# A fused SSD and GELU kernel: the long decay rows loaded from the GpSimd queue, w_out moved ahead in the load order, and a new order of all steps

## The chip, the cores and the metric

The kernel runs on one core of a Trainium2 chip. The metric is the device time of one launch in microseconds, as the median of repeated runs. The profile comes from one further execution, whose own time is given beside its span.

## The reference

Two stages follow each other. The first is a chunked state space recurrence over 4 batches, 8 heads and 768 positions with 32 values a head (`D`) and a state of 16 (`N`); the second is a feed-forward layer with a tanh-GELU on 3072 tokens of 256 values.

```python
cum = np.cumsum(la, axis=-1)
L = np.exp(cum[:, :, :, None] - cum[:, :, None, :])
...
CB = np.einsum('bhin,bhjn->bhij', Cc, Bc)
M = CB * L
y_intra = np.einsum('bhij,bhjd->bhid', M, xc)
decay_to_i = np.exp(cum)
y_inter = np.einsum('bhin,bhnd->bhid', Cc, state) * decay_to_i[:, :, :, None]
y[:, :, sl] = y_intra + y_inter
state = decay_full[:, :, None, None] * state + np.sum(Bx, axis=2)
...
h = x @ w_in
g = 0.5 * h * (1.0 + np.tanh(c * (h + 0.044715 * h * h * h)))
return (g @ w_out).astype(np.float32)
```

`a` (the decays) is needed before `B` and `C` can be scaled, these before any chunk can be computed, and `w_in` and `w_out` before its tokens can go through the feed-forward layer. The state runs through the 6 chunks of a batch in order.

## The kernel before, in words

The sequence is cut into 24 chunks of 128 positions, six for each batch. The first four chunks are units of their own (unit 0 to 3), the later ones go in pairs (units 4 to 13). Unit 4 holds the last two chunks of batch 0, units 5 to 7 are batch 1, and so on.

**Decays.** The rows of `a` for batch 0 come early and in short pieces (`a3_t`, two halves); those for batches 1 to 3 are the long rows, `a12_t`: `load_a12` (L164) brings them in four DMAs of 32 rows with 384 values, through `load_a` (L156, L157). VectorE clips them (`f_clip12`, L305), scans them into running products (`f_R12`, L301), transposes (`f_RT12`, L327) and takes reciprocals for each batch (L331).

**B and C.** Batch 0 comes in halves (`load_bc3`, L259); its scaled copies are made on VectorE (`f_mul3`, L361) and transposed on TensorE (`f_T3`, L372). Batches 1 to 3 come by `load_bc` (L153): B into the lower 64 partitions of one tile `bc_t`, C into the upper 64. One VectorE step `f_mul` (L400) scales both, so it needs both loads and the long decay rows; TensorE then transposes (`f_T`, L408), the results are copied out of PSUM (`f_E`), C is masked (`f_F`, L419), and B is transposed once more (`f_N`, L427, and `f_bn`).

**A unit** then takes `f_castx` (x to bf16), `f_G` (C times B, L462), `f_M` (the causal mask, VectorE, L472), `f_D` (the chunk's own state, L483), `f_S` (the running state, VectorE, L530 and L532), `f_SP` (the masked state, L539), `f_Y` (L505 from the state, L514 from the chunk itself) and `f_yev` (its copy to `xm`).

**Feed-forward.** `f_s1` (L563) multiplies by `w_in`, in groups that fill one PSUM bank: 8 matmuls of 128 columns for units 0 to 3, 4 matmuls of 256 columns later. ScalarE applies the GELU (L572). `f_s2` (L581) multiplies by `w_out`, 16 matmuls of 256 columns to a chunk, four of them to each quarter of `w_out`. `f_oev` (L588, L590) and `f_store` (L594) bring the result out. `w_in` (two loads of 1024 KB, L276) and `w_out` (four loads of 512 KB, L282) arrive in float32 in a pool of three buffers and are cast to bf16 in pieces of 512 columns on GpSimd or ScalarE (L288, L286).

**PSUM.** Groups of `f_s1` and the results of `f_D` share two banks (`hp`), so a result of `f_D` that VectorE has not read yet holds one of the two.

**The order.** No engine chooses at run time: each works off its own list in order. The lists come from a planner in the kernel (`run_order`), a list scheduler over nodes with an engine, an assumed duration, dependencies and a priority. The table `TUNE` overrides the priority of each node, `ENG` chooses the engine of those that have a choice, and the list `FIRST` with the loop after it gives the loads. All loads except six DMAs for `a3_t` on the ScalarE queue, and all stores, are issued from SyncE (SP), in the planner's order. Before the first `f_s1` group the planner fills idle TensorE time with dummy matmuls (L843).

Of the kernel before, what the change touches and what calls it, by code (L numbers as in the profile page):

```python
# [93 lines left out]
def kernel(  # L94
# [10 lines left out]
    nc = tc.nc  # L105
# [6 lines left out]
    HS = S // 2  # L112
    R3 = HS // 128
    R12 = S // 64
# [29 lines left out]
    a12_t = const.tile([128, HS], FP32, name="a12_t")  # L144
# [11 lines left out]
    def load_a(eng, o, at, n):  # L156
        eng.dma_start(out=o, in_=bass.AP(tensor=a.tensor, offset=a.offset + at,  # L157
                                         ap=[[S, batch * H], [1, n]]))
# [2 lines left out]
        n = ES if q == 3 else 2 * ES  # L161
        load_a(eng, a3_t[32 * q:32 * q + 32, i, 0:n], i * HS + q * ES, n)

    def load_a12():  # L164
        for q in range(4):
            load_a(nc.sync, a12_t[32 * q:32 * q + 32], (q % 2) * HS, HS)

    nc.vector.memset(a3_t[96:128, :, ES:], 1.0)
    for q in range(4):
# [424 lines left out]
        nc.sync.dma_start(out=out[gc * Q:(gc + 1) * Q, :], in_=outs.pop(gc))  # L594


    TUNE, ENG = {'ad_bc3_0_1': 14.089, 'ad_bc3_0_0': 14.0678, 'ad_wi_0': 14.1187, 'ad_x_0': 14.1183, 'ad_wi_1': 14.1056, 'ad_x_1': 14.1439, 'ad_bc3_1_1': 14.1458, 'ad_bc3_1_0': 14.1953, 'ad_x_2': 14.1853, 'ad_wo_0': 14.2062, 'ad_x_3': 14.2092, 'ad_wo_1': 14.2112, 'ad_wo_2': 14.2017, 'ad_wo_3': 14.2126, 'ad_a12': 14.1975, 'ad_x_4': 14.2621, 'ad_x_5': 14.2618, 'ad_bc_1_1': 14.2284, 'ad_bc_1_0': 14.2513, 'ad_x_6': 14.2822, 'ad_x_7': 14.3073, 'ad_x_8': 14.268, 'ad_x_9': 14.3453, 'ad_x_10': 14.2846, 'ad_x_11': 14.3005, 'ad_bc_2_1': 14.3163, 'wi_0_0': 21.0405, 'wi_0_1': 20.9083, 'wo_0_0': 20.9265, 'wo_0_1': 20.9062, 'wi_1_0': 20.9749, 'wi_1_1': 21.089, 'wo_1_0': 21.0332, 'wo_1_1': 20.9149, 'wi_2_0': 20.9485, 'wi_2_1': 21.0163, 'wo_2_0': 20.9335, 'wo_2_1': 20.9078, 'wi_3_0': 21.1114, 'wi_3_1': 20.9955, 'wo_3_0': 21.0099, 'wo_3_1': 21.0181, 'clip3_0': 21.0288, 'R3_0': 20.8079, 'RT3_0': 21.0102, 'recip3_0': 20.8186, 'mul3_0_1': 20.8335, 'mul3_0_0': 21.0695, 'pe_0': 20.7716, 'pp_0': 1064.0232, 'pend_0': 21.0365, 'clip3_1': 20.9727, 'R3_1': 21.0804, 'RT3_1': 21.0354, 'recip3_1': 21.0755, 'mul3_1_1': 21.0261, 'mul3_1_0': 20.899, 'pe_1': 21.012, 'pp_1': 1064.0555, 'pend_1': 20.9371, 'clip12': 20.9832, 'R12': 21.0475, 'RT12': 21.0619, 'recip12_1': 20.9625, 'recip12_2': 21.0472, 'recip12_3': 20.9963, 'castx_0': 21.0575, 'T3_0_1': 1064.1412, 'T3_0_0': 1064.0195, 'F0_0_0': 21.036, 'F0_0_1': 20.8627, 'E0_0': 20.8832, 'N_0_0': 1064.1682, 'bn_0_0': 20.789, 'G_0': 1064.1163, 'D_0': 1064.1738, 'M_0_0_0_2': 20.7953, 'M_0_0_2_4': 20.7659, 'S_0_0': 21.0221, 'SP_0': 21.0373, 'Y_0': 1064.1445, 'yev_0': 20.9328, 'castx_1': 20.9236, 'D_1': 1064.0368, 'M_1_0_0_4': 21.0544, 'S_1_0': 21.0483, 'SP_1': 21.0557, 'Y_1': 1064.1909, 'yev_1': 21.0776, 'castx_2': 20.9245, 'mul_1': 20.9712, 'T_1': 1063.9923, 'E_1_1': 20.9532, 'E_1_0': 20.8862, 'F_1': 21.0349, 'N_1': 1063.9691, 'G_2': 1064.0079, 'D_2': 1064.0093, 'M_2_0_0_4': 21.0354, 'S_2_0': 20.9225, 'SP_2': 21.0259, 'Y_2': 1064.1286, 'yev_2': 20.9261, 'castx_3': 20.9184, 'T3_1_1': 1064.0633, 'T3_1_0': 1063.994, 'F0_1_0': 20.9141, 'F0_1_1': 20.8485, 'E0_1': 21.0213, 'N_0_1': 1064.0256, 'bn_0_1': 21.0085, 'G_3': 1064.1608, 'D_3': 1063.9226, 'M_3_0_0_4': 21.0212, 'S_3_0': 20.9855, 'SP_3': 21.0435, 'Y_3': 1063.985, 'yev_3': 20.9136, 'castx_4': 20.9264, 'G_4': 1063.9808, 'D_4': 1063.9849, 'M_4_0_0_4': 20.9883, 'M_4_1_0_4': 21.0103, 'S_4_0': 21.0953, 'SP_4': 21.0283, 'Y_4': 1063.946, 'yev_4': 20.8422, 'castx_5': 20.8662, 'castx_6': 20.836, 'castx_7': 21.0818, 's1_0_0': 1064.0449, 'gelu_0_0': 20.8915, 's1_0_1': 1064.0631, 'gelu_0_1': 20.9213, 's1_0_2': 1064.0272, 'gelu_0_2': 20.8905, 's1_0_3': 1064.006, 'gelu_0_3': 21.0468, 's1_1_0': 1063.9464, 'gelu_1_0': 20.9289, 's1_1_1': 1064.0345, 'gelu_1_1': 20.8626, 's1_1_2': 1063.9974, 'gelu_1_2': 20.9102, 's1_1_3': 1063.8997, 'gelu_1_3': 20.8815, 's1_2_0': 1063.9713, 'gelu_2_0': 20.902, 's1_2_1': 1064.0101, 'gelu_2_1': 20.7947, 's1_2_2': 1063.9829, 'gelu_2_2': 20.8536, 's1_2_3': 1064.0064, 'gelu_2_3': 20.8901, 's1_3_0': 1063.9973, 'gelu_3_0': 20.9096, 's1_3_1': 1063.9988, 'gelu_3_1': 20.9607, 's1_3_2': 1063.9747, 'gelu_3_2': 20.9292, 's1_3_3': 1064.0169, 'gelu_3_3': 20.9948, 's1_4_0': 1063.8964, 'gelu_4_0': 20.9401, 's1_4_1': 1063.7613, 's2_0_0_0_o': 1064.1635, 's2_0_0_1_o': 1064.0266, 's2_0_0_2_o': 1064.0006, 's2_0_0_3_o': 1064.1858, 'oev_0': 20.8721, 's2_1_0_0_o': 1063.9561, 's2_1_0_1_o': 1063.9453, 's2_1_0_2_o': 1064.0086, 's2_1_0_3_o': 1064.0111, 'oev_1': 20.8661, 's2_2_0_0_o': 1063.9328, 's2_2_0_1_o': 1063.9913, 's2_2_0_2_o': 1064.0311, 's2_2_0_3_o': 1063.9668, 'oev_2': 21.0387, 's2_3_0_0_o': 1063.8998, 's2_3_0_1_o': 1063.8525, 's2_3_0_2_o': 1063.8591}, {'wi_0_1': 'ACT', 'wi_1_0': 'ACT', 'wo_1_1': 'ACT', 'wi_2_0': 'ACT', 'wo_2_0': 'ACT', 'wi_3_1': 'ACT', 'castx_0': 'ACT', 'F0_0_0': 'DVE', 'F0_0_1': 'DVE', 'E0_0': 'ACT', 'bn_0_0': 'DVE', 'castx_1': 'ACT', 'yev_1': 'DVE', 'E_1_1': 'ACT', 'E_1_0': 'ACT', 'bn_0_1': 'DVE', 'oev_2': 'DVE'}
    MERGE = UOF[CPB]
    TAIL = 4
    nodes = []  # L600
# [1 line left out]
    def add(eng, dur, fn, *args, deps=(), prio=0.0, done=None):  # L602

        name = "_".join([fn.__name__[2:]] + [str(v) for v in args])
        opts = eng if isinstance(eng, dict) else None
        if opts:
            eng = ENG.get(name, next(iter(opts)))
            dur = opts[eng]
            args = args + (eng,)
        n = Node(eng, dur, (lambda: fn(*args)), deps, TUNE.get(name, prio),  # L610
                 (0.26 if eng == "PE" else 0.0) if done is None else done)
        n.name, n.opts = name, opts
        nodes.append(n)
        return n
# [7 lines left out]
    def load(dur, fn, *args, deps=()):  # L622
        nload[0] += 1
        return add("DMA", dur, fn, *args, deps=deps, done=0.9, prio=nload[0])

    win_l, won_l, wi_n, wo_n = {}, {}, {}, {}
# [5 lines left out]
    a3n.done = 0.8  # L632
    a3n1 = add("SP", 7.2, landed, "a1", done=0.9, prio=-1)

    FIRST = "C30 B30 i0 x0 i1 x1 C31 B31 x2 o0 x3 o1 o2 o3 A x4 x5"
    for item in FIRST.split() + [f"{t}{b}" if t in "CB" else f"x{CPB * b + int(t)}"
                                 for b in range(1, batch) for t in "CB012345"]:
        t, i = item[0], int(item[1:] or 0)
        if t in "CB" and i >= 30:
            bl3[i - 30, int(t == "C")] = load(1.2, load_bc3, i - 30, int(t == "C"))  # L640
        elif t in "CB":
            bl[i, int(t == "C")] = load(1.2, load_bc, i, int(t == "C"))
        elif t == "A":
            a12n = load(1.7, load_a12)
        elif t == "x":
            xl[i] = load(1.0, load_x, i)
        elif t == "i":
            win_l[i] = load(2.65, load_wi, i)
        else:
            won_l[i] = load(1.35, load_wo, i)  # L650
# [11 lines left out]
    for k in range(2):  # L662
        z = 60.0 * k
        cl3n[k] = cl3 = add("DVE", 0.27, f_clip3, k, deps=[(a3n, a3n1)[k]], prio=-98 + z)
        R3n[k] = add("DVE", 0.55, f_R3, k, deps=[cl3], prio=-97 + z)
        RT3n[k] = add("DVE", 0.28, f_RT3, k, deps=[R3n[k]], prio=-96 + z)
        rc3[k] = add("DVE", 0.26, f_recip3, k, deps=[RT3n[k]], prio=-95 + z)
        mul3[k, 1] = add("DVE", 0.5, f_mul3, k, 1, deps=[bl3[k, 1], rc3[k]], prio=-94 + z)
        mul3[k, 0] = add("DVE", 0.5, f_mul3, k, 0, deps=[bl3[k, 0], RT3n[k]], prio=-93 + z)
        pen = add("DVE", 0.4, f_pe, k, deps=[R3n[k]], prio=-60 + z / 2)  # L670
        ppn = add("PE", 0.4, f_pp, k, deps=[pen], prio=-28)
        pendn[k] = add("ACT", 0.2, f_pend, k, deps=[ppn], prio=-29)
        ppn.takes("hp", pendn[k])
    cl12 = add("DVE", 0.42, f_clip12, deps=[a12n], prio=60)
    R12n = add("DVE", 1.08, f_R12, deps=[cl12], prio=60)
    RT12n = add("DVE", 1.02, f_RT12, deps=[R12n], prio=60)
# [44 lines left out]
    for u, cs in enumerate(UNITS):  # L721
        n = len(cs)
        q = 10.0 * cs[0]
# [16 lines left out]
        for k in range(n):  # L740
# [3 lines left out]
            else:  # L744
                ms.append(add("DVE", 1.24, f_M, u, k, 0, 4, deps=[gn] + ms,
                              prio=q + 1 + 0.1 * k if u > 1 else -16 + 2 * u + 0.1 * k))
# [8 lines left out]
        for k, gc in enumerate(cs):  # L755
            if gc % CPB == CPB - 1:
# [4 lines left out]
                          prio=q + 1.5 + 0.1 * k if u > 1 else -13.5 + u)  # L761
# [13 lines left out]
    for u, cs in enumerate(UNITS):  # L775
# [3 lines left out]
        for i in range(4 * n):  # L779
# [3 lines left out]
                              prio=PB + 10 * c0)  # L783
# [96 lines left out]
```

## Time and profile before

| | |
|---|---|
| median of 13 runs | 125.46 us (123.38 to 126.31) |
| time of the profiled execution | 126.11 us |
| its span, first to last instruction | 123.9 us |
| TensorE busy (matmul) | 112.2 us, 91% |
| ScalarE busy | 77.7 us, 63% |
| VectorE busy | 68.0 us, 55% |
| GpSimd busy | 17.4 us, 14% |
| read from HBM, written to it | 10.85 MB, 3.15 MB |
| the 24 x loads, each | 128 KB, median 4.7 us from issue to landing |
| the four w_out loads, each | 512 KB, median 5.7 us from issue to landing |
| the four loads of the long decay rows, each | 48 KB, median 2.1 us from issue to landing |
| clock granted to TensorE | full speed throughout |

The difference of the profiled execution's time to its span, 2.2 us, lies ahead of the first and after the last instruction. Engines with a "q" (SPq, PEq) are sequencers, which issue DMAs and wait. A wait is the idle time of an engine ahead of an instruction, with what ended it. The chain of waits is followed backwards from the last instruction, at each step to what released it.

### The profile page before, as it was taken

How to read it: one execution, taken by the hardware profiler on the slowest of the kernel's cores; microseconds unless marked ns; L12 is line 12 of the kernel's file. 1: busy time of each engine (PE TensorE's matmuls, PEld its weight loads, DVE VectorE, ACT ScalarE, POOL GpSimd, SP SyncE). 2: the span in 40 equal slices, each digit the busy share in tenths (PEclk: the TensorE clock that was granted, in tenths of full speed). 3: DMA queues.
4: the chain of work that ended last, by engine and by line, in shares of the span. 5: the costliest groups of instructions: out<-in, count | busy, mean ns of one | idle time of the engine just before them, and what ended most of it. 6: DMA issues, size and time to landing. Idle time of an engine off the chain costs nothing.

```text
span 123.9 us, 3597 instructions
## 1 busy us (share of the span) xinstructions
PE 112.2 (91%) x1537; PEld 98.8 (80%) x1537; DVE 68.0 (55%) x127; ACT 77.7 (63%) x150; POOL 17.4 (14%) x36
## 2 busy tenths in 40 slices
PE   5967997669899959999999999999999999999980
PEld 5946877468688848999888997979898899999960
DVE  5769979963939297852699461747557200000110
ACT  0516989464675647859766676776576877668510
POOL 7103506331331051011100000000000000000000
PEclk9999999999999999999999999999999999999999
DMA  1999979996879699995011101110111011111021
GB/s 41 204 366 354 160 212 330 320 200 108 162 187 227 111 163 240 149 166 138 0 42 48 42 0 48 42 45 3 45 42 48 7 40 42 42 42 42 9 81 42
DMA packets 37199, 14.23 MB, mean 115 GB/s; under 512 B 29952, under 2 KB 36416, under 8 KB 36928
## 3 DMA queue, kind: packets, MB, share of 16 engines
q1 hardware_dynamic: 36896, 13.87, 45.8%
q8 instruction: 12, 0.20, 0.7%
q10 hardware_dynamic: 288, 0.14, 0.6%
q14 instruction: 3, 0.02, 0.1%
HBM read 10.85 MB, written 3.15 MB: 113 GB/s over the span
## 4 chain that ended last, share of the span: by engine, by line
PE 61%; DMA 16%; SPq 13%; DVE 4%; ACT 1%; issue 1%; ACTq 0%; DVEq 0%
PE hp L563 26%; PE o_ps L581 24%; DMA bc_t<-in_B_dram 14%; SPq L268 4%; SPq L259 4%; DVE bc L400 3%; PE yb L581 3%; PE gb L462 2%; PE yb L505 2%; PE gb L408 2%; SPq L157 2%; DMA a_t<-in_a_dram 2%; PE yb L514 2%; SPq L282 1%; SPq L276 1%
## 5 line engine op out<-in xcount | busy, mean ns | idle before, releaser
L572 ACT ACTIVATE gT<-hp 128x512 bf16<-128x512 f32 x94 | 52.1, 596 | 18.1 <-PE hp L563 18.0
L563 PE MATMUL hp<-xm,w_in_sb 128*128 128x256 bf16 (+1 forms) x432 | 50.9, 259 | 1.4 <-DVE s_new L532 1.4
L581 PE MATMUL o_ps<-w_out_sb,gT 128*128 128x256 bf16 x352 | 46.9, 273 | 1.7 <-POOL w_out_sb L288 1.7
L563 PEld LDWEIGHTS <-w_in_sb 128*128 128x128 bf16 x448 | 42.0, 114 | 4.3 <-issue 3.3
L581 PEld LDWEIGHTS <-gT 128*128 128x128 bf16 x384 | 37.1, 98 | 6.3 <-issue 2.5
L472 DVE TENSOR_TENSOR m<-gb,tri 128x1024 bf16<-128x1024 f32 (+1 forms) x25 | 29.3, 1173 | 1.5 <-ACT gT L572 1.3
L590 DVE COPY o_sb<-o_ps 128x256 f32<-128x256 f32 x3 | 1.3, 425 | 23.6 <-ACT gT L572 19.5
L288 POOL CAST x<-x_t 128x512 bf16<-128x512 f32 (+1 forms) x12 | 8.0, 663 | 26.8 <-DMA x_t<-in_x_dram 20.9
L588 ACT ACTIVATE o_sb<-o_ps 128x256 f32<-128x256 f32 x19 | 7.3, 384 | 4.9 <-PE o_ps L581 2.7
L539 DVE SCALAR_TENSOR_TENSOR sp_new<-s_new,pend,bmask 128x256 bf16<-128x256 f32 x20 | 10.1, 506 | 0.1
L286 ACT ACTIVATE xm<-yb 128x512 bf16<-128x512 f32 (+1 forms) x13 | 7.1, 546 | 4.8 <-PE hp L483 3.7
L843 PEld LDWEIGHTS <-wz 128*128 128x128 bf16 x101 | 7.6, 114 | 2.9 <-DVE warm L178 1.5
L532 DVE SCALAR_TENSOR_TENSOR s_new<-s_new,pend,hp 128x64 f32<-128x64 f32 x16 | 4.5, 280 | 9.5 <-PE hp L483 9.2
L400 DVE TENSOR_TENSOR bc<-bc_t,rt 128x1536 bf16<-128x1536 f32 x3 | 5.3, 1755 | 5.1 <-DMA bc_t<-in_B_dram 5.1
L843 PE MATMUL yb<-wz 128*128 128x128 bf16 x63 | 5.4, 254 | 2.0 <-DVE warm L178 1.5
L514 PE MATMUL yb<-m,x 128*32 128x128 bf16 x192 | 6.3, 220 | 0.0
L505 PE MATMUL yb<-ce,sp_new 128*32 128x128 bf16 x160 | 5.4, 222 | 0.1
L462 PE MATMUL gb<-ce,bh 32*128 32x256 bf16 x96 | 4.9, 273 | 0.4 <-DVE bn L290 0.2
L288 POOL CAST w_out_sb<-wf 128x512 bf16<-128x512 f32 x6 | 4.0, 692 | 7.6 <-DMA wf<-in_moe_w_out_dram 7.6
L505 PEld LDWEIGHTS <-sp_new 128*32 128x32 bf16 x160 | 2.8, 96 | 1.9 <-issue 1.5
L514 PEld LDWEIGHTS <-x 128*32 128x32 bf16 x192 | 3.8, 97 | 0.6 <-issue 0.6
L581 PE MATMUL yb<-w_out_sb,gT 128*128 128x256 bf16 x32 | 4.0, 272 | 0.0
(78 smaller groups left out, 65.3 us busy)
## 6 DMA issues: line engine op xcount, KB each, us to landing
x_t<-in_x_dram SPq DMA_DIRECT2D x24, 128.0 KB, 4.7
out_dram<-o_sb SPq DMA_DIRECT2D x24, 128.0 KB, 1.7
wf<-in_moe_w_in_dram SPq DMA_DIRECT2D x2, 1024.0 KB, 7.3
wf<-in_moe_w_out_dram SPq DMA_DIRECT2D x4, 512.0 KB, 5.7
bc_t<-in_C_dram SPq DMA_DIRECT2D x3, 384.0 KB, 4.8
bc_t<-in_B_dram SPq DMA_DIRECT2D x3, 384.0 KB, 6.9
bc<-in_B_dram SPq DMA_DIRECT2D x2, 192.0 KB, 3.4
bc<-in_C_dram SPq DMA_DIRECT2D x2, 192.0 KB, 6.2
```

The costliest lines, as they stand in the source:

```text
L288: nc.gpsimd.tensor_copy(out=o, in_=i)
L400: nc.vector.tensor_tensor(out=d["bc16"], in0=d["bc"].rearrange("p h (r n) -> p r h n", r=R12), in1=w.rearrange("p r (h o) -> p r h o", o=1 ...
L462: nc.tensor.matmul(out=gb[:, g, 256 * k:256 * k + 256], lhsT=bh_of(gc)[32 * g:32 * g + 32], rhs=ce_of(gc)[32 * g:32 * g + 32], start=True, ...
L472: nc.vector.tensor_tensor(out=MT[gc][:, g0:g1], in0=gb[:, g0:g1, 256 * (k + half(u)):256 * (k + half(u)) + 256] .rearrange("p g (e t) -> p ...
L505: nc.tensor.matmul(out=y4[32 * j:32 * j + 32, k, w], lhsT=sp[:, 32 * h:32 * h + 32], rhs=ce_of(gc)[:, h % 2], start=first(j), stop=False, ...
L514: nc.tensor.matmul(out=y4[32 * j:32 * j + 32, k, w], lhsT=X16[u][:, k, 32 * h:32 * h + 32], rhs=m[:, h // 2, h % 2, :], start=first(j), st ...
L539: nc.vector.scalar_tensor_tensor(out=sp_new.rearrange("p (g d) -> p g d", g=4), in0=state[("s", gc)].rearrange("p (o d) -> p o d", o=1).to ...
L563: nc.tensor.matmul(out=hp[:, j * nt:(j + 1) * nt], lhsT=w_in_sb[:, kc].rearrange("p (q m k) -> p q k m", m=128, k=4) [:, fi // 4, fi % 4], ...
L572: nc.scalar.activation(gts[u][:, i * per:(i + 1) * per, 0:nt], hps.pop((u, i)).rearrange("p (j t) -> p j t", j=per), AF.Gelu_apprx_tanh)
L581: nc.tensor.matmul(out=ops[gc], lhsT=gts[u][:, fi, tt * Q:(tt + 1) * Q], rhs=w_out_sb[:, fi, :], start=(fi == 0), stop=(fi == NF - 1), ski ...
L588: nc.scalar.activation(o_sb, ops.pop(gc), AF.Copy)
L843: nc.tensor.matmul(out=(gb[:, 3] if g_next else yb)[:, 384:384 + w], lhsT=wz[:, 0:128], rhs=r, start=True, stop=True)
```

## The change

The four loads of the long decay rows leave SP's list and become four nodes on GpSimd, one behind the other, each planned to follow the first w_in load. In the load order w_out comes right behind x2, ahead of x3. Priorities of all nodes and some engine choices are new. The computation, the tiles and the buffers are the same.

```diff
-    def load_a12():
-        for q in range(4):
-            load_a(nc.sync, a12_t[32 * q:32 * q + 32], (q % 2) * HS, HS)
+    def f_a12(q):
+        load_a(nc.gpsimd, a12_t[32 * q:32 * q + 32], (q % 2) * HS, HS)
...
-    FIRST = "C30 B30 i0 x0 i1 x1 C31 B31 x2 o0 x3 o1 o2 o3 A x4 x5"
+    FIRST = "C30 B30 i0 x0 i1 x1 C31 B31 x2 o0 x3 o1 o2 o3 x4 x5"
...
-        elif t == "A":
-            a12n = load(1.7, load_a12)
...
+    a12n = None
+    for q in range(4):
+        a12n = add("POOL", 0.66, f_a12, q, deps=[a12n or win_l[1]], prio=15, done=2.5)
```

The rest of the diff is the line with `TUNE` and `ENG`, some 170 numbers. In `ENG` these steps change their engine: the first mask of C of batch 0 (`F0_0_0`), the copies `bn_0_0`, `bn_0_1`, `E0_1` and the result of chunk 2 (`oev_2`) go from VectorE to ScalarE; `bn` of batch 1 goes from ScalarE to VectorE; `castx_1` goes from ScalarE to GpSimd; ScalarE casts five pieces of w_in (four before) and one of w_out (two before), GpSimd three (four) and seven (six).

SP's list, from the built programs; x3 is the x load of chunk 3, B and C with a number are the whole batches, B0a and C0a the halves of batch 0, st a store:

```
before: a3 a3 B0a C0a w_in x0 w_in x1 C0b x2 B0b a12 a12 a12 a12 w_out w_out x3 w_out w_out
        C1 B1 x5 x4 x8 x6 x10 st x11 x7 st C2 x9 B2 st x12 ...
after:  a3 a3 C0a B0a w_in x0 w_in C0b B0b x1 x2 w_out w_out w_out w_out x3
        B1 C1 x4 x5 x7 st x6 x13 x15 x16 st x9 x8 x11 C2 x10 st x17 x14 B2 x12 st ...
```

GpSimd's list after its constants, in the same notation:

```
before: 4 w_in casts, castx_2, 3 w_out casts, castx_3, 3 w_out casts, castx_4 ...
after:  a12, 1 w_in cast, a12, a12, a12, 2 w_in casts, castx_1, castx_2, 7 w_out casts, castx_3, castx_4 ...
```

Elsewhere the lists move by a few places. On TensorE, `f_T` of batch 1 (L408) stood behind all 16 `f_s1` groups of units 0 to 3 and now stands behind 14 of them; between the first `f_s1` groups and that place the `f_s2` quarters of chunk 0 come earlier. On VectorE, the clip and scan of the long rows stand ahead of the `f_S` and the `f_yev` of unit 1, and the scaling of batch 2 (L400, the second) stands behind the masks of unit 6 and the running states of units 6 and 7, where it stood ahead of those masks and of the running states of unit 6. Line numbers after the change are one lower from L168 on.

## The prediction

> **What bounds the kernel now.** I read the page first, then the windows, the chain of waits in order of time, the waits and the timeline of the DMA queue. The page gives the chain's shares:
>
> ```profile
> PE 61%; DMA 16%; SPq 13%; DVE 4%; ACT 1%; issue 1%; ACTq 0%; DVEq 0%
> ```
>
> TensorE work is 61% of it, DMA and the DMA queue (SPq) 29%. The windows say where which holds. Their columns are the window, its length, the busy time of PE, PEld, DVE, ACT and POOL with counts, the clock, the DMA share and GB/s:
>
> ```profile
> 14.00:18.00 4.00, 3.89 (x88) 3.19 (x86) 3.60 (x8) 3.44 (x8) 0.44 (x2) 1.00 0.76 169
> 18.00:22.00 4.00, 3.17 (x50) 2.70 (x48) 3.63 (x7) 3.70 (x9) 2.24 (x3) 1.00 1.06 343
> 22.00:26.00 4.00, 3.03 (x53) 2.29 (x53) 3.70 (x6) 1.85 (x4) 1.03 (x3) 1.00 1.06 281
> 26.00:30.00 4.00, 3.10 (x41) 2.68 (x38) 1.10 (x2) 2.50 (x5) 1.17 (x2) 1.00 0.82 141
> ...
> 42.00:46.00 4.00, 2.65 (x57) 2.09 (x50) 3.28 (x4) 1.46 (x3) 1.16 (x2) 1.00 0.70 110
> 46.00:50.00 4.00, 4.00 (x74) 3.32 (x72) 3.17 (x6) 2.87 (x7) 1.01 (x2) 1.00 0.97 234
> ```
>
> From 46 us to the end TensorE has no idle time: the windows to 110 us all show it busy in full, and nothing there can be won by another order. The first GELU matmuls start at 13.39. Between there and 46 us its idle time is 0.11 + 0.83 + 0.97 + 0.90 from the first four lines, 0.32 in 30:34, 0.02 in 34:38 and 1.35 in 42:46: 4.5 us. That is the most that the change can bring, unless the feed-forward starts earlier. The chain names what these gaps hang on (start, length, what):
>
> ```profile
> 19.19 10.44 DMA bc_t<-in_B_dram
> 29.65 0.05 DVEq L400
> 29.70 0.04 issue
> 29.75 1.77 DVE bc L400
> 31.51 0.05 issue
> 31.56 0.86 PE gb L408 x12
> ...
> 35.70 6.90 DMA bc_t<-in_B_dram
> 42.64 0.04 issue
> 42.68 1.76 DVE bc L400
> ```
>
> B of batch 1 is issued at 19.19, lands at 29.63, is scaled on VectorE and transposed (L408) at 31.56. B of batch 2 lands at 42.6 and VectorE scales it at once. Behind that scaling stand the running states of unit 6 (L532), whose inputs hold a PSUM bank: this is the 1.35 us gap. The waits (total, times, longest) give it, and those for w_out:
>
> ```profile
> PE o_ps L581 <- POOL w_out_sb L288: 1.7, 4, 0.7
> PE hp L563 <- DVE s_new L532: 1.4, 1, 1.4
> ```
>
> The queue's timeline shows the loads of the long decay rows in the way:
>
> ```profile
> 13.66 2.19 SPq L157 DMA_DIRECT2D a_t<-in_a_dram  x4
> 15.89 0.90 SPq L282 DMA_DIRECT2D wf<-in_moe_w_out_dram  x2
> ```
>
> w_out is issued 2.23 us after the last load of batch 0, and in the window 14:18 the 16 DMA engines are at 0.76, against 1.01 to 1.06 in the windows around: 0.24 x 4 = 0.96 us of DMA time is lost.
>
> **What the Trainium skill says.** Its page "DMA: Bandwidth & Descriptors", section "Issuing engines are not separate DMA queues": another issuing engine saves only issue time, the 16 DMA engines are shared. The trace agrees as far as it goes: 2.19 us of issue, and the engines full around it. So the change can give back about the 0.96 us, not the transfers. The same page, section "Anatomy of one DMA — SWDGE (gpsimd) path": some 2.0 us of fixed cost for a DMA from GpSimd. Before, no DMA comes from there; the same rows from SP took 2.1 us to land. The Trainium skill's page "SBUF — State Buffer", section "A bandwidth-pool intuition that's wrong": VectorE can hold the port through which GpSimd writes descriptors, and a DMA of 0.62 us then took 3.1 us. No row of the trace shows it; I price it as a rival. Its page "TensorE: Matmul & The Clock Gate", Part 1: the clock falls after some 3.4 us without work. The trace shows no fall, and no gap after 13 us over 1.35 us.
>
> **The change part by part.**
>
> *Long rows on GpSimd.* On SP, four issues go, 2.23 us, and w_out follows batch 0's last loads directly. The DMA engines carry the same bytes. Gain for whatever lands behind them: at most 2.2 us (issue bound), at least 0 (the idle time comes back elsewhere); I take the 0.96 us of idle DMA time, 1.0.
>
> On GpSimd, one issue falls into idle time (its constants end at 3.84, its next work is at 9.53). The other three stand between its first w_in cast (9.53 + 0.6 = 10.1) and the next, whose w_in lands at 12.6: room of 2.5 us, 0.83 each. The trace has no such issue; SP's took 0.42 to 0.8, the planner assumes 0.66. Between 0.5 (nothing is delayed) and 3.1 (the Trainium skill's blocked case), I take 0.8: nothing. They land, with 2 us, at about 14.6. VectorE now clips them (L305 before) after the scaling of batch 0's second half, which by its rows, from 9.1 on (the second half's `a3_t` lands at 8.19, clip and scan follow), 0.68 + 0.34 + 0.68 + 0.30 + 1.18 + 0.21 + 0.29 + 0.47 + 1.22 + 0.56 + 0.55 from 9.1 takes 6.5 us to 15.6: no wait, 1.0 us spare. Behind the clip stand the scan (0.96), the running state and `f_yev` of unit 1, which gates its GELU matmuls.
>
> *w_out ahead of x3.* Its four loads landed at 19.45 to 26.95. Issued 2.2 us earlier and in one run of 1.34 us each, they land at about 17.4 to 21.5; the 1.7 us of waits for their casts go. x3 moves from 22.5 to about 23.5, still ahead of the place where TensorE wants it, since three more quarters of `f_s2` (12 x 0.109 = 1.3 us) now come before it. But all this lies ahead of L408, and L408 waits for batch 1. So it counts only as cover: TensorE gets to L408 sooner and waits longer there, some 2 us.
>
> *B and C of batch 1.* Between w_in and them the queue has the same loads as before, so they land 1.0 us earlier, 28.6; scaling 28.7 to 30.5, L408 at 30.55 in place of 31.56: 1.0 us won.
>
> *The new order of TensorE.* Ahead of L408 now stand 14, not 16, of the groups of units 0 to 3. Two groups, 16 matmuls of 0.061 us, 0.97 us, therefore come after it. Before, from L408 to the first group of unit 4 took 35.24 - 31.56 = 3.68 us, of it about 0.2 waiting, which they can fill: 0.8 us lost. The work is the same, but it can't be done in the wait any more.
>
> *The scaling of batch 2.* It now stands behind the running states of units 6 and 7 and behind unit 6's masks, so nothing that TensorE needs soon waits for B2: the 1.35 us go. B2 itself comes later: 13 x loads stand between B1/C1 and it, not 8, five more at about 0.8 us (six in a row landed from 43.20 to 47.16), so 42.6 - 1.0 + 4.0 + one store 0.4 = 46.0. Then 1.76 scaling, 1.22 + 0.47 + 1.22 for unit 7's masks, and T of batch 2, which before came at 53.15 and would now come at about 51.6, may run from 50.7: 0.9 us spare, loss 0. If B2 lands 2 us later still, 1.1 us are lost.
>
> *Engine choices.* First mask and copies of batch 0 in parallel on two engines, C first: the first G moves from 8.7 to about 8.2, but the first GELU matmul waits for w_in (12.6 + cast 0.7 = 13.3). Nothing. Should w_in land later, by the 0.9 us over which these rows landed (16.54 to 17.42), the 2 us wait at L408 hides that too.
>
> Sum on the profiled execution: -1.0 + 0.8 - 1.35 = -1.55; 126.11 becomes 124.55, its span 123.9 becomes 122.35. The median of the runs is 0.65 lower than the profiled one; with the same step it becomes 123.9.
>
> **The rivals.**
> A. *Forecast*, 123.9: for it speak the dense TensorE after 46 us and the named gap at 42:46. Chance 0.5, range of its own 123.0 to 124.9.
> B. *Batch 1 lands no sooner*: the idle DMA time comes back as slow short packets or the rows now take their share ahead of w_in. Then 0 + 0.8 - 1.35: 124.9, no change that counts. The window 18:30, where the DMA engines are full and still B takes 10.4 us, speaks for it. Chance 0.25.
> C. *Batch 1 lands by the full 2.2 us sooner*: L408 at 29.35, -2.2 + 0.8 - 1.35 = -2.75, 122.7; should the two late groups be hidden as well, -3.55, 121.9. Against it: the engines are full. Chance 0.12.
> D. *Slower*: GpSimd's three issues each wait for VectorE. At 3.1 us each the next w_in cast starts at 10.1 + 9.3 = 19.4 in place of 12.65, 6.75 late; the wait at L408 hides 2.0, the rest comes on top: +4.75 - 1.55 + 1.0 (rows and w_out gain nothing then) = +4.2, 129.7. It decides from (2.5 + 2.0) / 3 = 1.5 us each on; from about 2.0 the kernel is slower than before. VectorE is busy for 3.97 of the 4 us in 10:14, but mostly with operations that read PSUM. Chance 0.13, also with the milder 126.5.
>
> **How the numbers follow.** Runs of this kernel spread over 2.9 us, so what is within 1% (1.25 us) counts as no change. Faster by more than that (below 124.2): two thirds of A, all of C, a little of B, together 0.5. Same: the rest of A and most of B, 0.36. Slower: D and a little of B, 0.14. The range takes in A, C's first value and B's worse end, and leaves out most of D: 122.3 to 126.3.
>
> **What would show it.** Right: DMA share near 1 in 14:18; `bc_t` of batch 1 landing near 28.6 with a wait of TensorE for L400 ahead of L408 of about 2 us; no wait for L288 ahead of L581; no gap near 44; no gap in 46:110. Wrong: the first L563 later than 14.5, VectorE waiting for the long rows at its clip, TensorE waiting ahead of the second L408, or a granted clock below 1.

## The result, and the profile after

| | before | after |
|---|---|---|
| median of the runs | 125.54 us (48 runs, 123.38 to 128.0) | 123.42 us (11 runs, 122.65 to 126.08) |
| ratio, 95% interval | | 0.9894 [0.9853, 0.9934] |
| profiled execution, its span | 126.11, 123.9 us | 123.42, 121.5 us |

Forecast was 123.9 with a range of 122.3 to 126.3. The ratios, here and below, leave out runs more than 1.5% above the fastest of the same kernel, the medians and means take all runs, so the two can differ.

The profile after, read in the order of the prediction. The page's shares of the chain:

```profile
PE 72%; SPq 13%; DMA 9%; DVE 2%; issue 1%; ACTq 0%; DVEq 0%
```

TensorE carries 72% of the chain, not 61%, and transfers 9%, not 16%. The windows, with the same columns as before:

```profile
14.00:18.00 4.00, 3.18 (x64) 2.74 (x65) 3.92 (x7) 3.69 (x8) 1.85 (x3) 1.00 0.88 202
18.00:22.00 4.00, 3.82 (x71) 3.21 (x71) 3.77 (x7) 2.89 (x7) 2.94 (x6) 1.00 1.00 392
...
42.00:46.00 4.00, 4.00 (x73) 3.36 (x71) 2.84 (x5) 3.16 (x7) 0.91 (x3) 1.00 1.10 251
46.00:50.00 4.00, 4.00 (x39) 3.81 (x37) 3.87 (x4) 3.17 (x7) 1.68 (x1) 1.00 1.01 168
```

The gap in 42:46 is gone. The DMA share in 14:18 rose from 0.76 to 0.88, which is half of the idle time that the forecast wanted back. The chain (start, length, what) on the way to T of batch 1, and its waits (total, times, longest):

```profile
19.09 9.12 DMA bc_t<-in_C_dram
28.33 1.77 DVE bc L399
30.14 0.84 PE gb L407 x12
```

```profile
PE gb L407 <- DVE bc L399: 1.0, 1, 1.0
PE yb L513 <- POOL x L287: 0.7, 1, 0.7
```

The last load that T of batch 1 needs, now C, lands at 28.21 in place of 29.63, T starts at 30.14 in place of 31.56. TensorE waits for it 1.0 us, and 0.7 us for the cast of x3 ahead of unit 3's Y. GpSimd's timeline shows the new issues (start, length), SP's what follows from them:

```profile
3.80 0.64 POOL L157 DMA_DIRECT2D a_t<-in_a_dram  x1
10.13 0.60 POOL L287 CAST w_in_sb<-wf 128x512 bf16<-128x512 f32 x1 [5.69 <-DMA wf<-in_moe_w_in_dram]
10.69 1.47 POOL L157 DMA_DIRECT2D a_t<-in_a_dram  x3
```

```profile
14.05 2.89 SPq L281 DMA_DIRECT2D wf<-in_moe_w_out_dram  x4
16.99 0.51 SPq L267 DMA_DIRECT2D x_t<-in_x_dram  x1
17.55 1.50 SPq L153 DMA_DIRECT2D bc_t<-in_B_dram  x1
```

The rows land at 10.4 and 15.6 to 15.9, the clip follows at 16.12 without a wait. w_out is issued 1.84 us sooner and the first batch load 0.86 us sooner (18.41 before).

### The profile page after: what moved, and what is told of

The parts are those of the page before. It is cut to its first block, busy times and chain, and to the rows that moved or that the text cites. A ratio compares the mean times of both kernels' runs of the same rounds, so it can differ in the third digit from the quotient of the medians.

```text
span 121.5 us, 3600 instructions
## 1 busy us (share of the span) xinstructions
PE 111.9 (92%) x1535; PEld 99.6 (82%) x1535; DVE 66.3 (55%) x123; ACT 79.1 (65%) x153; POOL 21.0 (17%) x41
## 4 chain that ended last, share of the span: by engine, by line
PE 72%; SPq 13%; DMA 9%; DVE 2%; issue 1%; ACTq 0%; DVEq 0%
PE hp L562 31%; PE o_ps L580 29%; DMA bc_t<-in_C_dram 8%; SPq L267 4%; PE yb L580 3%; SPq L258 3%; PE gb L461 2%; SPq L281 2%; PE yb L504 2%; PE yb L513 2%; SPq L275 2%; PE gb L407 2%; DMA a_t<-in_a_dram 2%; DVE bc L399 1%; SPq L153 1%; PE gb L426 1%
## 5 line engine op out<-in xcount | busy, mean ns | idle before, releaser
L562 PE MATMUL hp<-xm,w_in_sb 128*128 128x256 bf16 (+1 forms) x432 | 51.6, 260 | 0.0
L580 PE MATMUL o_ps<-w_out_sb,gT 128*128 128x256 bf16 x352 | 47.4, 273 | 0.1
L287 POOL CAST x<-x_t 128x512 bf16<-128x512 f32 (+1 forms) x13 | 10.1, 777 | 28.1 <-DMA x_t<-in_x_dram 17.8
L589 DVE COPY o_sb<-o_ps 128x256 f32<-128x256 f32 x2 | 0.8, 423 | 23.0 <-ACT gT L571 19.5
L843 PEld LDWEIGHTS <-wz 128*128 128x128 bf16 x99 | 8.2, 122 | 3.5 <-issue 1.7
L843 PE MATMUL yb<-wz 128*128 128x128 bf16 x61 | 6.3, 276 | 2.5 <-DVE warm L177 1.6
L285 ACT ACTIVATE w_in_sb<-wf 128x512 bf16<-128x512 f32 x5 | 3.0, 623 | 2.0 <-DMA wf<-in_moe_w_in_dram 2.0
L529 DVE COPY s_new<-hp 128x64 f32<-128x64 f32 x4 | 0.9, 222 | 6.2 <-PE hp L482 6.2
## 6 DMA issues: line engine op xcount, KB each, us to landing
x_t<-in_x_dram SPq DMA_DIRECT2D x24, 128.0 KB, 4.8
out_dram<-o_sb SPq DMA_DIRECT2D x24, 128.0 KB, 1.7
```

The costliest lines, as they stand in the source:

```text
L285: nc.scalar.activation(o, i, AF.Copy)
L287: nc.gpsimd.tensor_copy(out=o, in_=i)
L562: nc.tensor.matmul(out=hp[:, j * nt:(j + 1) * nt], lhsT=w_in_sb[:, kc].rearrange("p (q m k) -> p q k m", m=128, k=4) [:, fi // 4, fi % 4], ...
L580: nc.tensor.matmul(out=ops[gc], lhsT=gts[u][:, fi, tt * Q:(tt + 1) * Q], rhs=w_out_sb[:, fi, :], start=(fi == 0), stop=(fi == NF - 1), ski ...
L843: nc.tensor.matmul(out=(gb[:, 3] if g_next else yb)[:, 384:384 + w], lhsT=wz[:, 0:128], rhs=r, start=True, stop=True)
```

## A single profile is one draw

The accounts of the two profiles seem to close: T of batch 1 (its transposes on TensorE, L408 before, L407 now) starts 1.42 us sooner and the gap of 1.35 us is gone, less 0.5 us for the new order, which makes 2.3 us; the ends of TensorE's work differ by 2.2 (118.00, 120.22). The runs below do not bear this out, so a second profile of each kernel, unchanged, comes first.

> The kernel before, unchanged, for a second profile. The scaling of batch 2 moved alone won 0.4 to 0.5 us, where 1.35 was forecast from one profile. Theory (that profile had B2 late): here B2 lands less than 11.0 us after T of batch 1 has started, 9 to 10 us after it, and the gap near 44 is 0.3 to 0.8 us in place of 1.35. Rival (the gap is always there, and moving the scaling only shifts the wait): the gap is 1.3 to 1.4 us again.

> The changed kernel, unchanged, timed beside the next two. Theory: -1.7 to -2.2 us, ratio 0.985 to 0.990; in its profile no gap near 44, T of batch 1 (L407) 1.5 to 2.2 us ahead of the 31.56 of the kernel before, with a wait of 0.5 to 1.2 us there.

The kernel before, profiled again, took 123.90 us. Its wait for L532 near 44 is not there; in 42:46 TensorE is busy in full, and the scaling of batch 2 starts at 40.09, not at 42.68 (window; timeline of VectorE):

```profile
42.00:46.00 4.00, 4.00 (x44) 3.67 (x36) 3.52 (x6) 3.39 (x7) 1.31 (x3) 1.00 0.99 178
```

```profile
40.09 1.76 DVE L400 TENSOR_TENSOR bc<-bc_t,rt 128x1536 bf16<-128x1536 f32 x1 [0.28 <-DMA bc_t<-in_B_dram]
```

B2 landed at 39.99 in place of 42.59, which is 9.0 us after the start of T of batch 1 in place of 11.0. T started at 30.95. So the gap is not a fixed property of that program: it was open in one profile and closed in the other. Its size, expected at 0.3 to 0.8 us, was 0.

The changed kernel's second look had a mean of 123.74 us in 6 runs (ratio 0.9894 [0.9824, 0.9964]). Its profiled execution took 124.96 us; the last load for T landed at 29.52, T started at 31.46. T had been expected 1.5 to 2.2 us ahead of the 31.56 of the kernel before; it came 0.1 us ahead. The first w_out load was issued at 15.13 and the first load of batch 1 at 18.13, only 0.76 and 0.28 us sooner than in the kernel before. The waits of TensorE in 13 to 33.5 us that concern loads:

```profile
PE gb L407 <- DVE bc L399: 1.1, 1, 1.1
PE o_ps L580 <- ACT w_out_sb L285: 1.1, 1, 1.1
PE hp L482 <- POOL x L287: 1.0, 1, 1.0
```

A wait for w_out of 1.1 us, which the first profile of this kernel did not have, stands here; that for x3 is not here (the third line is an earlier x load). The DMA share in 14:18 is no steadier. The second profiles of the kernel before and of the changed kernel, in this order, show the same 0.79:

```profile
14.00:18.00 4.00, 3.88 (x88) 3.19 (x86) 3.43 (x8) 3.46 (x7) 0.46 (x1) 1.00 0.79 186
14.00:18.00 4.00, 2.98 (x47) 2.49 (x45) 3.39 (x5) 3.78 (x8) 2.20 (x4) 1.00 0.79 170
```

What lands when differs between two executions of one program by 0.6 to 2.6 us in these four profiles (B of batch 1 before 29.62 and 29.01, C after 28.21 and 29.52, B2 before 42.59 and 39.99), as much as the whole effect. The parts are therefore priced by times of many runs, and the profiles used for the mechanism.

One number is steady in the profiles: from the start of T of batch 1 to the end of TensorE's work. In the old order, where there is no gap near 44, it is 87.2, 87.3, 87.2 and 87.2 us (b_again, e2, e5, e10), in the changed kernel 87.9 and 88.1. With the gap it was 88.7 in the kernel before. This interval does not say when T starts.

## Experiments

Each moves a step in the finished list of the planner (`behind`, `ahead`: take a step out and put it behind or ahead of another); all other steps keep their order. Results, against runs of the kernel before on the same chip (the second set of the changed kernel stands above):

| run | runs | median | mean against before, 95% interval | ratio, 95% interval |
|---|---|---|---|---|
| changed kernel | 11 | 123.42 | -1.6 [-2.3, -0.9] | 0.9894 [0.9853, 0.9934] |
| e1 rows on GpSimd | 22 | 123.53 | -1.7 [-2.1, -1.3] | 0.9858 [0.9824, 0.9893] |
| e2 scaling later | 22 | 124.81 | -0.5 [-1.0, 0.0] | 0.9948 [0.9908, 0.9988] |
| e5 both | 22 | 123.32 | -1.9 [-2.2, -1.6] | 0.9891 [0.9864, 0.9919] |
| e4 changed, rows on SP | 22 | 125.34 | +0.1 [-0.3, 0.5] | 1.0009 [0.9975, 1.0043] |
| e9 B2 later | 6 | 129.10 | +3.9 [3.1, 4.6] | 1.0275 [1.0173, 1.0377] |
| e10 B2 and scaling later | 22 | 124.54 | -0.3 [-0.6, 0.0] | 1.0025 [0.9996, 1.0054] |
| e3 changed, x3 amid w_out | 22 | 124.21 | -0.2 [-1.0, 0.6] | 0.9892 [0.9864, 0.9921] |
| e7 changed, waits filled | 6 | 123.15 | -1.6 [-2.2, -0.8] | 0.9863 [0.9811, 0.9915] |
| e11 changed, rows behind cast | 22 | 123.54 | -1.2 [-1.6, -0.7] | 0.9935 [0.9903, 0.9967] |
| e12 filled, rows behind cast | 22 | 123.56 | -1.4 [-1.8, -1.0] | 0.9937 [0.9903, 0.9970] |

The ratio of e9 rests on two runs. Where means and ratios say different things, both are given below, and the size is then open between them.

**Parts alone and together: e1, e2, e5.** My theory was: two parts, each alone worth its term. Rivals: the new order as a whole, or w_out ahead of x3.

```diff
-            load_a(nc.sync, a12_t[32 * q:32 * q + 32], (q % 2) * HS, HS)
+            load_a(nc.gpsimd, a12_t[32 * q:32 * q + 32], (q % 2) * HS, HS)
...
+    ahead("ad_a12", "wi_0_0")
```

> The kernel before, with only the four loads of the long rows issued from GpSimd, between its first two and its last two w_in casts; every other list as before. Theory (less in SP's queue): w_out and B and C of batch 1 are issued about 2.2 us sooner and land about 1.4 us sooner, so B near 28.2 and L408 near 30.1 in place of 31.56; the gap of 1.35 us near 44 stays. Time -1.0 to -1.4 us, ratio 0.989 to 0.992. Rival (all comes from the new order): 0, ratio 0.997 to 1.003. Rival (w_out sooner is what pays): also faster, but because the 1.7 us of waits ahead of L581 go, with L408 where it was.

```diff
+    behind("mul_2", "SP_9")
```

> The kernel before, with only the scaling of batch 2 (the second L400) moved on VectorE behind the masks of unit 6 and the running states of units 6 and 7. Theory: the gap of 1.35 us ahead of the L563 that waits for L532 near 44 goes, no other comes, since B2 has landed at 42.6 and T of batch 2 is wanted only near 52: -1.0 to -1.35 us, ratio 0.989 to 0.992. Rival: the wait moves to T of batch 2 or to unit 7's masks, and the ratio is 0.997 to 1.003.

The place is one step earlier than in the changed kernel: in e2's trace the scaling (45.27) stands behind unit 6's masks and running states but ahead of unit 7's running state (L532 at 46.94), which the changed kernel has at 45.04, ahead of the scaling at 45.45. The same holds for e5 and e10. e5 has both edits.

> Both edits at once in the kernel before: the long rows from GpSimd, and the scaling of batch 2 later; TensorE's list as before. Theory: the two add, about -2.4 to -2.75 us, ratio 0.978 to 0.981, so it is as fast as the changed kernel or up to 0.5 us faster, since the two groups stand in front of T of batch 1 as they did. Rival (the new order of TensorE is needed): at most -1.35, ratio 0.989 or above.

The rows alone give the whole gain, more than expected, by the mean (1.7 us) and by the ratio (1.8). The scaling alone gives about half of what was expected, 0.5 by the mean and 0.65 by the ratio. Both together give 1.9 by the mean and 1.4 by the ratio: beside the rows the scaling adds 0.25 us [-0.2, 0.65] by the means and takes 0.4 away by the ratios, so nothing is shown for it there. With the scaling later in both, the rows are worth 1.4 us [0.9, 1.9] by the means on one chip (e5 against e2) and 0.7 by the ratios. The rival of the new order falls with e1, which has TensorE's old list and all the gain (e5's ratio of 0.9891 on its own would have fitted that rival, 0.989 or above). The rival that w_out pays falls too: its last quarter landed at 26.60 in e1, between the 26.95 and 26.34 of the kernel before, and the wait for it is as long as it was:

```profile
PE o_ps L581 <- POOL w_out_sb L288: 1.7, 3, 1.0
```

In e1 SP's timeline shows how the queue gives back less than the four issues:

```profile
13.85 1.92 SPq L282 DMA_DIRECT2D wf<-in_moe_w_out_dram  x2
15.81 0.43 SPq L268 DMA_DIRECT2D x_t<-in_x_dram  x1
16.29 1.40 SPq L282 DMA_DIRECT2D wf<-in_moe_w_out_dram  x2
17.73 0.71 SPq L153 DMA_DIRECT2D bc_t<-in_C_dram  x1
18.49 0.69 SPq L153 DMA_DIRECT2D bc_t<-in_B_dram  x1
```

The first two w_out issues take 1.92 us where they took 0.90, so B is issued 0.70 us sooner than before (19.19), not 2.2. It landed at 28.86. T of batch 1 started at 31.56, 30.95, 30.75, 31.80 and 31.97 in the five profiles with the old order and the rows on SP, on average 31.4, and at 30.80 and 30.63 in the two with the rows on GpSimd: 0.7 sooner. But on one chip there is no such difference: 30.75 in e2, 30.80 in e1, 30.63 in e5. The times say 0.7 to 1.8 us. So that the rows' place gives the gain is shown by the times; the way from SP's queue to the sooner end is not traced. That the rows themselves land sooner (by 16.12, not by 17.42) is not it: VectorE clips them at 18.96 in e1 and at 18.84 in the kernel before. In e1 T did not wait for B at all, and the chain on the way to it runs over w_out, which shows how close the two are:

```profile
16.91 9.68 DMA wf<-in_moe_w_out_dram
```

The gap for L532 was 0.56 us in e1; that it is smaller there because B2 also lands sooner is likely, but two profiles do not settle it.

**The undo: e4.** The changed kernel with the rows behind x2 on SP.

```diff
-        load_a(nc.gpsimd, a12_t[32 * q:32 * q + 32], (q % 2) * HS, HS)
+        load_a(nc.sync, a12_t[32 * q:32 * q + 32], (q % 2) * HS, HS)
...
+    behind("a12_0", "ad_x_2")
+    behind("a12_1", "a12_0")
+    behind("a12_2", "a12_1")
+    behind("a12_3", "a12_2")
```

> The changed kernel, with only the four loads of the long rows put back on SP, behind x2 and ahead of w_out; all other lists as in the changed kernel. Theory: B and C of batch 1 are issued 2.2 us later and land 1 to 1.4 us later, T of batch 1 (L407) near 31.3 in place of 30.1, TensorE's wait there grows from 1.0 to about 2.2 us; the time is 1.0 to 1.4 us above the changed kernel, ratio to the kernel before 0.992 to 1.002. Rival (all comes from the new order): no later than the changed kernel, 0.989.

The size came as expected: the gain is gone. The path did not. The last load landed at 30.23 and its scaling ended at 32.11, but T started at 33.71, with no wait: TensorE itself was late. Wait, and windows of 2 us:

```profile
PE o_ps L580 <- ACT w_out_sb L285: 1.8, 1, 1.8
```

```profile
26.00:28.00 2.00, 0.94 (x12) 0.84 (x11) 0.83 (x1) 1.62 (x4) 0.62 (x1) 1.00 1.11 191
28.00:30.00 2.00, 1.90 (x30) 1.42 (x28) 0.00 (x0) 1.48 (x4) 0.40 (x1) 0.72 0.57 105
30.00:32.00 2.00, 2.00 (x15) 1.63 (x14) 1.65 (x1) 0.29 (x1) 0.72 (x1) 0.50 0.67 139
```

The last quarter of w_out landed at 26.36 (22.58 in the changed kernel), f_s2 waited 1.8 us for its cast, and then the clock fell to half for some 3 us. In the changed order of TensorE, w_out can thus be what T waits behind. (In the second profile of the changed kernel it landed at 24.86.) VectorE waited too, for the rows at their clip, which in this order stands early; of the two waits of this line the one at 17.75, of 1.0 us, is that for the long rows:

```profile
DVE ac L304 <- DMA a_t<-in_a_dram: 2.2, 2, 1.2
```

So e4 does not price SP's queue alone: the new order was made for early rows. And its profiled execution, 127.11 us, was the longest of the 22 (median 125.34); how much of these waits the others had is open. The loss itself does not need the drop of the clock: the five executions with a mean granted clock of 1.00 took 124.39 to 125.34 us.

**Is the place of the scaling worth anything: e9, e10.** B2 alone is put later, then the scaling too.

```diff
+    behind("ad_bc_2_0", "ad_x_13")
```

> The kernel before, with only the load of B of batch 2 put behind a store and two x loads on SP; the scaling of batch 2 in its old place, ahead of the running states of unit 6. Theory (the old place costs what B2 is late, from about 41.2 us on; B2 landed at 42.6 with a gap of 1.35 us in one profile of the kernel before and at 40.0 with none in the other): B2 lands at 42.5 to 44 us, the gap ahead of L563 is 1.2 to 2.8 us, time +0.7 to +2 us, ratio 1.005 to 1.016. Rival (the place of the scaling does not matter): ratio 0.997 to 1.003.

> The same late B2, with the scaling of batch 2 behind the masks of unit 6 and the running states of units 6 and 7. Theory: no gap near 44, T of batch 2 does not wait; the time is that of the move of the scaling alone (-0.4 to -0.6 us, ratio 0.995), 1.2 us or more below the run with B2 late and the scaling in its old place. Rival: like that run, within 0.4 us.

In e9 B2 landed at 44.79. The waits, and windows of 2 us:

```profile
PE hp L563 <- DVE s_new L532: 3.2, 1, 3.2
```

```profile
44.00:46.00 2.00, 0.00 (x0) 0.00 (x0) 1.19 (x1) 0.19 (x1) 0.38 (x1) 1.00 0.55 86
46.00:48.00 2.00, 0.77 (x4) 0.60 (x5) 1.96 (x4) 0.00 (x0) 1.53 (x2) 0.67 0.81 180
48.00:50.00 2.00, 2.00 (x12) 1.40 (x10) 2.00 (x4) 1.21 (x3) 0.13 (x1) 0.50 1.06 276
```

The gap is 3.2 us where at most 2.8 was expected, and the time rose by 3.9 us by the mean and 3.4 by the ratio, where at most 2 was expected: TensorE's clock is at half in 48:50, and from T of batch 1 to the end it now takes 91.9 us, which is 87.2 + 3.2 and another 1.5. Five of the six runs had a mean granted clock of 0.984 to 0.987, as the profiled one (129.50 us); the one at 1.00 took 127.14. In e10 B2 landed at 44.16 and TensorE had no gap:

```profile
42.00:46.00 4.00, 4.00 (x70) 3.41 (x69) 3.05 (x5) 2.68 (x7) 1.23 (x2) 1.00 0.83 132
```

Against the kernel before, e10 is 0.3 us below by the mean and 0.3 above by the ratio (1.0025), where 0.4 to 0.6 below was expected. The same move of the scaling that wins 0.5 us or nothing when B2 comes as it did wins 4.2 us [3.4, 4.8] by the means, 3.1 by the ratios, when B2 is late. In the changed kernel B2 lands at 45.43 and 45.95, later still: there the move most likely is what keeps the late B2 from costing time, but no run undoes it there.

**w_out's place: e3.** In the changed kernel x3 goes back between the second and third w_out load.

```diff
+    ahead("ad_x_3", "ad_wo_2")
+    ahead("castx_3", "wo_2_0")
```

> The changed kernel, with x3 loaded between the second and the third w_out load, as before the change, and its cast ahead of those of the third quarter. Theory (the place of w_out is cover, T of batch 1 waits for B and C either way): the 0.7 us wait for x3 goes, w_out's third and fourth quarter land 0.3 to 0.8 us later and make waits of about as much, L407 is where it was: within 0.4 us of the changed kernel. Rival (w_out first is what pays): 0.8 us or more slower than the changed kernel, ratio 0.994 or above.

By the ratio nothing changed, as expected. Its runs reach to 130.28 us, which pulls up the mean of all; the ten with a mean granted clock below 0.99 took 122.78 to 130.28 us, the other twelve 122.67 to 124.91. Its profile has a wait of 1.5 us for w_out. Whether x3's place matters stays open.

**Can the two waits be filled: e7, e11, e12.**

```diff
+    ahead("s2_2_0_0_o", "T_1")
+    ahead("s2_2_0_1_o", "T_1")
+    behind("Y_3", "s2_1_0_0_o")
+    behind("s1_3_0", "s2_1_0_2_o")
```

> The changed kernel, with four steps of TensorE moved: two quarters of f_s2 of chunk 2 ahead of T of batch 1, and unit 3's Y behind the first quarter of chunk 1's f_s2 with the first group of unit 3 two quarters later. Theory (these waits of 1.0 us for B and C and of 0.7 us for x3 are on the path, since nothing waits again before the end): 0.9 to 1.6 us below the changed kernel, ratio to the kernel before 0.974 to 0.981. Rival (a later wait, for the running states, the copies after T of batch 1 or T of batch 2, takes the place): within 0.4 us of the changed kernel.

e11 has the next edit alone, e12 has it together with the four above.

```diff
+    behind("a12_0", "wi_0_1")
```

> The changed kernel, with the first of the four loads of the long rows issued behind the first w_in cast on GpSimd, with the other three, and not at 3.8 us. Theory: w_in lands 0.3 to 0.6 us sooner and the first L562 starts as much sooner (13.4 to 13.7 in place of 14.05 and 14.59), but the wait ahead of L407 takes it: within 0.4 us of the changed kernel, ratio 0.986 to 0.992. Rival (the start is on the path): 0.5 us or more below the changed kernel, ratio 0.985 or less.

> The changed kernel, with the four moved steps of TensorE (two quarters of f_s2 of chunk 2 ahead of T of batch 1, unit 3's Y and first group later) and all four row loads behind the first w_in cast. Theory (B and C of batch 1 set the pace up to 31 us): 0.5 to 1.2 us below the changed kernel, ratio 0.979 to 0.986, and no slower than the filled version alone (0.9863). Rival: within 0.4 us of the changed kernel.

e7 was 0.4 us below the changed kernel on its chip [-1.25, 0.6], e12 0.2 below e11 [-0.6, 0.2], so neither gain is shown; e12's ratio, expected no higher than e7's 0.9863, was 0.9937. In e7 and e12, T to the end is 87.4 us in place of 87.9, so 0.5 us of work was indeed pulled into the wait; but T started at 30.71 and 32.12, when the loads had landed at 28.77 and 30.18, and in e12 another wait of 2.3 us for w_out stood ahead of it. The expected 0.9 to 1.6 us did not come. e11's mean is that of the second set of the changed kernel (-1.2), as expected, though its ratio came out above the expected span; its w_in landed at 13.19, no sooner than the 13.21 of the changed kernel, but in e12, with the same row loads, it landed at 11.87 (13.87 in the changed kernel's second profile, 13.02 in e7). Whether the early row load delays w_in stays open. e12's first GELU matmul started at 12.78, 1.2 us ahead of e7's, and the time gained nothing by it. No version here is shown to beat e1, which is the old order with the rows on another queue.

## Why the prediction was right, and where it was not

The forecast of 123.9 and the direction held. Of its three terms one, the scaling, was clearly mis-sized, and one, the rows, probably, in opposite directions; that they nearly cancel, and so the closeness of 123.4 to 123.9, is luck.

**Rows off SP's queue, -1.0.** Right in kind and probably too small: 1.7 us by the mean and 1.8 by the ratio in the old order; with the scaling later 1.4 [0.9, 1.9] by the mean and 0.7 by the ratio; between e4 and the changed kernel 1.4 [0.7, 2.1], which comes from another set of runs and takes in VectorE's wait. The path of the working is not confirmed. It took the idle DMA time of 14:18, of which half came back in one profile of the changed kernel and nothing in the other; T of batch 1, forecast at 30.55, started at 30.14 and 31.46. The working also held that only B and C count and all that lies ahead of L408 is cover. That failed in e4, and in e1's profile, where the chain to T runs over w_out: the last w_out quarter can be later than B and C for TensorE.

**The two moved groups, +0.8.** Right: from T of batch 1 to the end the changed order takes 87.9 to 88.1 us, the old one 87.2: +0.7 to +0.9. The 0.2 us of waiting that the working took off is not in the trace: from 31.56 to 35.24 TensorE is busy in full. The times show the term less clearly: the changed kernel's ratio, 0.9894, is that of e5, 0.9891, which has the rows and the scaling in the old order; by the means of its two sets it is 0.3 to 0.7 us above e5, which ran beside other runs of the kernel before.

**The scaling of batch 2, -1.35.** This is the term that was wrong in size: measured alone -0.5 [-1.0, 0.0] by the mean and -0.65 by the ratio, and beside the rows nothing clear. The step "this is the 1.35 us gap" took a wait of one profile for one of every run; in the second profile of the same kernel it is absent. The size would follow if the gap were open in part of the executions, but two profiles cannot show how often it is. Sum with the terms by the means: -1.4 + 0.7 - 0.5 = -1.2; measured -1.6 [-2.3, -0.9] and, in the second set of runs, -1.2 [-2.0, -0.5].

**The smaller steps.** GpSimd's issues were priced at 0.8 us and took 0.64 for a first and 0.50 for each next one, while VectorE was busy for 3.97 of the 4 us of 10:14 in e1. The fear of rival D, drawn from the Trainium skill's "SBUF — State Buffer", section "A bandwidth-pool intuition that's wrong" (VectorE can hold the port), has no support in this trace; most of VectorE's work between 10.7 and 12.8 there were masks, which read PSUM, so the page's own case, a copy on VectorE, is not tested. The rows landed at 15.6 to 15.9, not at 14.6: 4.3 to 4.9 us after their issue, where 2.0 was assumed; the clip did not wait, as forecast. w_out, forecast to land from 17.4 to 21.5, landed from 18.68 to 22.58, and from 19.18 to 24.86 in the second profile. x3 came at 25.0, not at 23.5, and made a wait of 0.7 us in one profile. The start of the feed-forward, forecast without change, was 0.7 us later (14.05; 14.59 in the second profile); TensorE still waited at T afterwards, as the text's condition had it. That wait was 1.0 and 1.1, not 2. Two signs that the prediction named for being wrong did show: this start later than 14.5, in one of two profiles, and a granted clock below 1, with a mean of 0.968 to 0.986 in 5 of the 12 executions on record. B2 was forecast at 46.0 and landed at 45.43 and 45.95, and T of batch 2 had no wait.

**The rivals.** B in its time (the rows give nothing) falls with e1 and e4; that batch 1 lands sooner is not settled, as the second profile of the changed kernel and the profiles of one chip show. Its argument was also read too high: the DMA engines were at 1.06, 1.06 and 0.82 in 18:30, not full to the end. C (the full 2.2 us) does not hold either: in e1 B was issued 0.7 us sooner, and the rows are worth 0.7 to 1.8 us. D falls with the issue durations.

## What to carry over

A gap in one profile should be priced only when a second execution shows it too: here the largest term of the sum was in one of two. The same goes for a path that one profile seems to show. Taking issues off a queue can pay less in issue time than they took: here 2.2 us of them went and the load behind them was issued 0.7 us sooner, because the issues between took longer. It still was the whole gain. A step that waits for a late load should not stand in front of work that frees a PSUM bank; what that is worth depends on how late the load is, here from at most about 0.5 us to 3 or 4.

## What the hardware showed that was not expected

TensorE's clock. The Trainium skill's page "TensorE: Matmul & The Clock Gate", Part 1, gives about 3.4 us of idleness before the clock halves. In e9 it fell sooner, inside the gap of 3.2 us: with 0.50 from the fall on, as in 48:50, the mean of 0.67 in 46:48 puts the fall near 46.7, which is 2.7 us after TensorE's last work ended (43.99). In e4 the longest wait was 1.8 us, with TensorE busy for 2.09 of the 4 us in 24:28, and the clock still was at 0.50 in 30:32: a sparse stretch can do it, without a gap of that length. It need not do it: in e12 TensorE was busy for 0.80 of the 3.41 us from 22.55, with a wait of 2.3 us, and the clock stayed at 1.00. What decides is not shown.

How often the clock fell differs between the versions. A mean granted clock below 0.99 (one stretch at half, as in e4's profile, gives 0.983) stands in 17 of 22 runs of e4, 10 of 22 of e3, 6 of 22 of e11 and 5 of 12 of the changed kernel, against 15 of 75 of the kernel before, 1 of 22 of e5 and none of 22 of e1. In e11 the runs with it took 124.4 us on average, the others 123.4.

Landing times. B2 of the same program landed at 42.59 and 39.99, and the last load for T of batch 1 in the changed kernel at 28.21 and 29.52.
